# A fused attention, expert and dense kernel: the dense layer's token blocks change from six of 384 to 512, 256, 512, 512 and 512

## The chip, the cores and the metric

The kernel runs on one core of one Trainium2 chip. The metric is the device time of one execution in microseconds (us). Runs of the kernel before took 822.37 to 823.5 us, with a median of 822.54.

## What is computed

Four batches of eight heads go through windowed attention, the 2304 resulting tokens of 512 features through a layer of eight experts (each token to one), and every token through a dense layer with 2048 hidden features. Cut to what matters here, the last part is:

```python
def _moe2_ref(x, w_in, w_out):          # x: 2304 x 512
    h = x @ w_in                        # 512 x 2048
    beta = 1.0
    neg = h <= -beta
    pos = h >= beta
    g = np.where(pos, h, np.where(neg, 0.0, (h + beta) ** 2 / (4.0 * beta)))
    return (g @ w_out).astype(np.float32)   # 2048 x 512
```

w_in and w_out come as 64-bit floats; the kernel turns them into pairs of 32-bit values itself.

## The kernel before

There are three stages in one program. Attention and routing come first. Then the experts go one after another, largest first; expert e holds up to `CAPS[e]` tokens (384 down to 256), and its output, turned so that features lie on the partitions, is written to `ysT` in device memory, the tokens sorted by expert. The dense layer reads `ysT` in blocks of tokens. Last, rows are scattered to their places in the output by indirect DMA.

Every product is made of three matmuls: each operand is split into a high and a low part (`yh`/`yl`, `wc..h`/`wc..l`, `gh`/`gl`), and high by high, high by low and low by high are added up in PSUM.

**The dense layer before.** The 2304 tokens are six blocks of 384 (`HT`). The hidden features are 16 chunks of 128 (`ff`). A step of a block and a chunk has a first-layer part, `in_part` (L1532): 4 x 3 matmuls of 384 columns into a PSUM tile `ch` (L1539 to L1541), of which there are two, used in turn. Behind it stands the activation, as a chain over two engines: ScalarE makes `r` (L1545), VectorE squares it (L1547) and takes the maximum with `ch` (L1549), ScalarE rounds to `gh` (L1550), VectorE subtracts for `gl` (L1553). The chain's maximum is the last reader of `ch`. The second-layer part, `out_part` (L1576), has for each 128 tokens three matmuls of 512 columns that add to an output bank `o` (L1565 to L1567); there are six output banks. After chunk 15, `put` (L1578) copies a bank to SBUF, on ScalarE for even and on VectorE for odd tiles, and GpSimd issues the scatter (L1584).

The blocks go in four runs, the first two of two blocks each:

```python
    RUNS = (((0, 1), 0, 1), ((2, 3), 0, 1), ((4,), 0, 2), ((5,), TH, 2))
```

The last number of a run is its lag: the second-layer part of a chunk is issued so many chunks behind its first-layer part. The order on TensorE within a step of a pair is so: first-layer part of one block, of the other, then both second-layer parts of the chunk before. At the very start there is no chunk before, so four first-layer parts stand in a row.

A block is loaded by `load_y` (L1126, on the sync engine's DMA queue) and split into high and low parts by `split_y` (L1130, one ScalarE and one VectorE pass for each of four pieces).

**The conversion of the weights.** `conv64` (L1045) converts the 16 chunks of w_in and w_out. Half a chunk (w_in or w_out) costs VectorE four passes (L1059, L1061, L1064, L1052) and ScalarE two (`cvr`, L1043, and `wc..h`, L1067). It is a generator: what calls `next` on it sets where these passes stand in the queues. The first `NEARLY` = 5 chunks are converted during the expert stage, by `side_work` (L1393), two or three pieces for each hidden chunk of an expert. The others are advanced by `more` (L1527), five pieces in each `in_part` from the third on, so that one chunk is converted in each step of the first pair. The raw weights wait in two buffers; the load for two halves ahead is issued behind a half's second pass.

`py` is the pool of three buffers in which the experts' turned inputs (`new_xT`) and the dense blocks take turns.

Of the kernel before, what the change touches and what calls it, by code (L numbers as in the profile page):

```python
# [9 lines left out]
F32 = mybir.dt.float32  # L10
F32R = mybir.dt.float32r
BF16 = mybir.dt.bfloat16
I32 = mybir.dt.int32
# [7 lines left out]
P = 128  # L21
B, H, S, D = 4, 8, 576, 64
N = B * S
DM = H * D
E = 8
F = 1024
FF = 2048
# [3 lines left out]
CAP = 384  # L31
CAPS = (384, 376, 344, 314, 296, 286, 274, 256)
L2, L3 = 2, 4
NRAW, NW, LEAD = 6, 7, 5
NEARLY = 5
BIAS = {"V": 1.2}
# [11 lines left out]
CT = CAP // P  # L48
GT, HT = 768, 384
QF = S - S % P  # L50
# [6 lines left out]
def f(ap):  # L57
    return ap.bitcast(F32)
# [3 lines left out]
def fused_kernel(ctx, tc, qk, vT, v, emb, tau, w1, w2, win64, wout64, out):  # L62
    nc = tc.nc
# [957 lines left out]
    pcv = pool(ctx, "pcv", 1)  # L1021
    py = pool(ctx, "py", 3)
    wch = {}
# [97 lines left out]

    yt = {}

    def load_y(i):
        yl = py.tile([P, 4, CAP], F32R, tag="xl", name="yl")
        yh = py.tile([P, 4, CAP], F32R, tag="xh", name="yh")  # L1126
        nc.sync.dma_start(f(yl), ysT[:, i * HT:(i + 1) * HT].rearrange("(c p) s -> p c s", p=P))
        yt[i] = (yh, yl)
# [8 lines left out]
    with ExitStack() as bb:  # L1137
        pw = pool(bb, "pw", NW)
        px = pool(bb, "px", 2)
# [141 lines left out]
        def new_xT():  # L1281
            xh = py.tile([P, 4, CAP], F32R, tag="xh", name="xh")
            xl = py.tile([P, 4, CAP], F32R, tag="xl", name="xl")
            return xh, xl
# [229 lines left out]
    pg = pool(ctx, "pg", 3)  # L1514
    po = pool(ctx, "po", 2)
    ps_h = pool(ctx, "ps_ch", 2, space=PSUM)
# [4 lines left out]
    cv = conv64(range(NEARLY, FF // P), pcl)  # L1521
    TH = HT // P

    RUNS = (((0, 1), 0, 1), ((2, 3), 0, 1), ((4,), 0, 2), ((5,), TH, 2))
    outs, parts = {}, [0]

# [5 lines left out]
    def in_part(hf, ff):  # L1532
        parts[0] += 1
        w1h, w1l = wch[ff][:2]
        yh, yl = yt[hf]
        hp = ps_h.tile([P, HT], F32, tag="ch", name="ch")
        for c in range(4):
            o = slice(c * P, (c + 1) * P)
            nc.tensor.matmul(hp, w1h[:, o], yh[:, c], start=(c == 0), stop=False)  # L1539
            nc.tensor.matmul(hp, w1h[:, o], yl[:, c], start=False, stop=False)  # L1540
            nc.tensor.matmul(hp, w1l[:, o], yh[:, c], start=False, stop=(c == 3))  # L1541
        r = pg.tile([P, HT], F32, tag="r", name="r", bufs=2)
        a = pg.tile([P, HT], F32R, tag="gh", name="gh", bufs=4)
        b = pg.tile([P, HT], F32R, tag="gl", name="gl", bufs=4)
        nc.scalar.activation(r, hp, AF.Relu, bias=halfc, scale=0.5)  # L1545
        more()
        nc.vector.scalar_tensor_tensor(r, r, 1.0, r, op0=ALU.min, op1=ALU.mult)  # L1547
        more()
        nc.vector.tensor_tensor(r, hp, r, op=ALU.max)  # L1549
        nc.scalar.activation(a, r, AF.Copy)  # L1550
        more()
        more()
        nc.vector.tensor_tensor(b, r, f(a), op=ALU.subtract)  # L1553
        more()
        return a, b

    def out_tile(run, ff, gs, i, t):
        halves, b0, _ = run
        _, _, w2h, w2l = wch[ff]
        hf = halves[i]  # L1560
        gh, gl = gs[i]
        if ff == 0:
            outs[hf, t] = ps_o.tile([P, DM], F32, tag=f"o{b0 + i * TH + t}", name=f"o{b0 + i * TH + t}")
        o, out_ = slice(t * P, (t + 1) * P), outs[hf, t]
        nc.tensor.matmul(out_, gh[:, o], w2h, start=(ff == 0), stop=False)  # L1565
        nc.tensor.matmul(out_, gl[:, o], w2h, start=False, stop=False)  # L1566
        nc.tensor.matmul(out_, gh[:, o], w2l, start=False, stop=(ff == FF // P - 1))  # L1567
        if ff == FF // P - 1:
            put(hf, t)

    def out_part(run, ff, gs):
        for i in range(len(gs)):
            for t in range(TH):
                out_tile(run, ff, gs, i, t)

    def put(hf, t):  # L1576
        ot = po.tile([P, DM], F32, tag="ot", name="ot", bufs=3)
        if t % 2 == 0:  # L1578
            nc.scalar.activation(ot, outs.pop((hf, t)), AF.Copy)  # L1579
        else:  # L1580
            nc.vector.tensor_copy(ot, outs.pop((hf, t)))
        k = hf * TH + t
        nc.gpsimd.memset(gap, 0.0)  # L1583
# [6 lines left out]
    for run in RUNS:  # L1590
        halves, _, lag = run
        ahead = [h for h in (halves[0] + 2, halves[0] + 3) if len(halves) == 2 and h < N // HT]
        if ahead:
            load_y(ahead[0])
            coming = split_y(ahead[0])
        for ff in range(FF // P):
            gs = []
            for hf in halves:
                gs.append(in_part(hf, ff))
                if ahead and ff == FF // P - 1 and hf == halves[0]:  # L1600
                    del yt[hf]
                    load_y(ahead[1])
            todo.append((run, ff, gs))
            while len(todo) > lag:
                out_part(*todo.pop(0))
            if ff in (11, 12, 13, 14):
                next(coming, None)
        if ahead:
            for _ in split_y(ahead[1]):
                pass  # L1610

    for n, t in ((0, 0), (1, 0), (0, 1), (1, 1), (0, 2), (1, 2)):
        out_tile(*todo[n], 0, t)

# [44 lines left out]
```

## Time and profile before

| what | before |
|---|---|
| median of three runs | 822.54 us |
| profiled execution, its own time | 822.19 us |
| its span, first to last instruction | 820.5 us |
| TensorE busy, of the span | 806.9 us, 98% |
| weight loads busy | 749.8 us, 91% |
| VectorE busy | 516.9 us, 63% |
| ScalarE busy | 421.5 us, 51% |
| GpSimd busy | 137.7 us, 17% |
| mean granted clock of TensorE | 0.999 |

A busy time is the time in which at least one instruction of an engine ran. Matmuls overlap, and their ends are modelled, so a TensorE that is busy all the time can still lose time between the starts of its matmuls: starts are what to read. The names PE, DVE, ACT and POOL in the rows are TensorE, VectorE, ScalarE and GpSimd.

### The profile page before, as it was taken

The page shows a single profiled execution, that of the slowest core. Times are in us where ns is not written, and L with a number is a line of the kernel's source. Part 1 is how long each engine was busy: PE and PEld are TensorE (multiplying, and loading weights), DVE is VectorE, ACT ScalarE, POOL GpSimd, SP SyncE. Part 2 cuts the span into 40 slices and gives each one's busy share as a digit, 9 for nine tenths or more (in the row PEclk, how much of TensorE's full clock was granted, in tenths as well). Part 3 has the DMA queues.
Part 4 walks back from the last instruction along what each step waited for, and adds up shares of the span by engine and source line. Part 5 has one row for each costly group of instructions (what it writes and reads, how often), then busy time and mean ns, then how long its engine had stood idle before and what let it go on. Part 6 is the DMA issues. An engine that isn't in the chain of part 4 may idle for free.

```text
span 820.5 us, 14256 instructions
## 1 busy us (share of the span) xinstructions
PE 806.9 (98%) x5242; PEld 749.8 (91%) x5242; DVE 516.9 (63%) x1390; ACT 421.5 (51%) x881; POOL 137.7 (17%) x205
## 2 busy tenths in 40 slices
PE   9999999999999999999999999999999999999996
PEld 7999999869999999999998989999999999999995
DVE  7777767897667687777469898544343454344332
ACT  7879899856435466566345555333222333223221
POOL 5975664031110110100000000011000003001001
PEclk9999999999999999999999999999999999999999
DMA  9846942648645668776134332021000012001001
GB/s 335 308 158 237 330 160 71 227 160 277 202 159 166 216 216 276 241 235 198 62 116 128 129 122 84 1 100 55 0 1 1 1 40 77 1 1 40 1 0 39
DMA packets 59180, 106.03 MB, mean 129 GB/s; under 512 B 3942, under 2 KB 35686, under 8 KB 59104
## 3 DMA queue, kind: packets, MB, share of 16 engines
q1 hardware_dynamic: 55776, 95.15, 34.7%
q0 software_dynamic: 3328, 9.90, 3.5%
q8 instruction: 43, 0.70, 0.3%
q14 instruction: 33, 0.27, 0.1%
HBM read 90.42 MB, written 14.62 MB: 128 GB/s over the span
## 4 chain that ended last, share of the span: by engine, by line
issue 56%; PE 12%; POOL 2%; ACT 0%; DVE 0%; POOLq 0%; ACTq 0%
PE bh L1458 2%; POOL out L1584 2%; PE bh L1460 2%; PE bh L1459 2%; PE by L1447 2%; PE by L1449 2%; PE by L1448 2%; PE bx L1295 1%; ACT whi L555 0%; DVE wlo L560 0%; POOL gap L1583 0%; PE permp L1385 0%; POOLq L1655 0%; POOL xg L1166 0%; ACT yo L1497 0%
## 5 line engine op out<-in xcount | busy, mean ns | idle before, releaser
L1547 DVE SCALAR_TENSOR_TENSOR r<-r 128x384 f32<-128x384 f32 x96 | 53.4, 556 | 120.6 <-ACT r L1545 117.1
L1539 PE MATMUL ch<-yh,wc_0h 128*128 128x384 f32 x384 | 129.2, 336 | 0.0
L1541 PE MATMUL ch<-yh,wc_0l 128*128 128x384 f32 x384 | 129.1, 336 | 0.0
L1540 PE MATMUL ch<-yl,wc_0h 128*128 128x384 f32 x384 | 128.7, 335 | 0.0
L1545 ACT ACTIVATE r<-ch,halfc 128x384 f32<-128x384 f32 x96 | 55.2, 575 | 117.4 <-PE ch L1541 117.1
L1550 ACT ACTIVATE gh<-r 128x384 fp32r<-128x384 f32 x96 | 50.5, 526 | 123.4 <-DVE r L1549 123.4
L1566 PE MATMUL o<-wc_1h,gl 128*128 128x512 f32 x288 | 113.3, 393 | 0.1
L1567 PE MATMUL o<-wc_1l,gh 128*128 128x512 f32 x288 | 113.3, 393 | 0.0
L1565 PE MATMUL o<-wc_1h,gh 128*128 128x512 f32 x288 | 112.0, 389 | 0.0
L1584 POOL DMA_INDIRECT out<-ot,permu x18 | 17.5, 973 | 462.2 <-ACT ot L1579 458.9
L560 DVE TENSOR_TENSOR wlo<-wraw,whi 128x1024 fp32r<-128x1024 f32 x64 | 78.0, 1222 | 20.1 <-ACT whi L555 19.6
L1553 DVE TENSOR_TENSOR gl<-r,gh 128x384 fp32r<-128x384 f32 x96 | 53.4, 557 | 43.7 <-ACT gh L1550 42.6
L1458 PE MATMUL bh<-xh,whi 128*128 128x256 f32 (+6 forms) x256 | 80.2, 313 | 0.0
L1448 PE MATMUL by<-hl,whi 128*128 128x256 f32 (+6 forms) x256 | 77.5, 303 | 1.8 <-DVE hl L1464 1.8
L1447 PE MATMUL by<-hh,whi 128*128 128x256 f32 (+6 forms) x256 | 77.3, 302 | 0.0
L1449 PE MATMUL by<-hh,wlo 128*128 128x256 f32 (+6 forms) x256 | 77.3, 302 | 0.0
L1460 PE MATMUL bh<-xh,wlo 128*128 128x256 f32 (+6 forms) x256 | 77.1, 301 | 0.0
L1459 PE MATMUL bh<-xl,whi 128*128 128x256 f32 (+6 forms) x256 | 76.9, 301 | 0.0
L1539 PEld LDWEIGHTS ch<-yh,wc_0h 128*128 128x128 f32 x384 | 72.1, 188 | 2.9 <-DVE r L1549 0.3
L1540 PEld LDWEIGHTS ch<-yl,wc_0h 128*128 128x128 f32 x384 | 72.1, 188 | 2.5
L1541 PEld LDWEIGHTS ch<-yh,wc_0l 128*128 128x128 f32 x384 | 72.0, 188 | 0.0
L555 ACT ACTIVATE whi<-wraw 128x1024 fp32r<-128x1024 f32 x64 | 67.3, 1055 | 0.7 <-ACTq L1476 0.7
(270 smaller groups left out, 1718.9 us busy)
## 6 DMA issues: line engine op xcount, KB each, us to landing
wraw<-in_w SPq DMA_DIRECT2D x64, 512.0 KB, 4.6
rqk<-in_qk SPq DMA_DIRECT2D x30, 576.0 KB, 5.1
raw<-in_w_in SPq DMA_DIRECT2D x16, 512.0 KB
raw<-in_w_out SPq DMA_DIRECT2D x16, 512.0 KB, 4.7
vT<-in_vT SPq DMA_DIRECT2D x16, 288.0 KB, 2.8
yl<-ysT SPq DMA_DIRECT2D x6, 768.0 KB, 6.0
x_dram<-xt SPq DMA_DIRECT2D x8, 512.0 KB, 6.6
vt<-in_v SPq DMA_DIRECT2D x8, 438.0 KB, 6.8
```

Of the source, the lines that this page charges most:

```text
L1447: nc.tensor.matmul(y, w2h[:, o], hh[:, :cap], start=(ff == 0), stop=False)
L1448: nc.tensor.matmul(y, w2h[:, o], hl[:, :cap], start=False, stop=False)
L1449: nc.tensor.matmul(y, w2l[:, o], hh[:, :cap], start=False, stop=(ff == 7))
L1458: nc.tensor.matmul(hp, w1h[:, o], xh[:, c, :cap], start=(c == 0), stop=False)
L1459: nc.tensor.matmul(hp, w1h[:, o], xl[:, c, :cap], start=False, stop=False)
L1460: nc.tensor.matmul(hp, w1l[:, o], xh[:, c, :cap], start=False, stop=(c == 3))
L1539: nc.tensor.matmul(hp, w1h[:, o], yh[:, c], start=(c == 0), stop=False)
L1540: nc.tensor.matmul(hp, w1h[:, o], yl[:, c], start=False, stop=False)
L1541: nc.tensor.matmul(hp, w1l[:, o], yh[:, c], start=False, stop=(c == 3))
L1565: nc.tensor.matmul(out_, gh[:, o], w2h, start=(ff == 0), stop=False)
L1566: nc.tensor.matmul(out_, gl[:, o], w2h, start=False, stop=False)
L1567: nc.tensor.matmul(out_, gh[:, o], w2l, start=False, stop=(ff == FF // P - 1))
```

## The change

The dense layer gets five blocks of 512, 256, 512, 512 and 512 tokens. The first run has the blocks 0 and 1, the other runs one block each, with lag 1, the last with lag 2. Only 3 chunks of weights are converted in the expert stage. The experts' turned inputs move from `py` to the pool `px`; blocks get places of their own, the blocks 0 and 3 one, 1 one, 2 and 4 one in a pool `pz` that takes space the expert stage has left. The activations get two buffers for each block width, and in the last run four slots in the place of the blocks 0 and 3. The output copies use the conversion's `cvr` and `cva` buffers, two each, instead of three of their own. The six output banks are used in a circle over all 18 tiles of tokens.

```diff
-NEARLY = 5
+NEARLY = 3
...
-GT, HT = 768, 384
+SIZES = (512, 256, 512, 512, 512)
+GT = max(SIZES)
...
-    py = pool(ctx, "py", 3)
+    py = pool(ctx, "py", 1)
...
     def load_y(i):
-        yl = py.tile([P, 4, CAP], F32R, tag="xl", name="yl")
-        yh = py.tile([P, 4, CAP], F32R, tag="xh", name="yh")
-        nc.sync.dma_start(f(yl), ysT[:, i * HT:(i + 1) * HT].rearrange("(c p) s -> p c s", p=P))
+        t0, n = sum(SIZES[:i]), SIZES[i]
+        place, tag = ((py, 0), (py, 1), (late[0], 2), (py, 0), (late[0], 2))[i]
+        yl = place.tile([P, 4, n], F32R, tag=f"yl{tag}", name="yl")
+        yh = place.tile([P, 4, n], F32R, tag=f"yh{tag}", name="yh")
+        nc.sync.dma_start(f(yl), ysT[:, t0:t0 + n].rearrange("(c p) s -> p c s", p=P))
...
         def new_xT():
-            xh = py.tile([P, 4, CAP], F32R, tag="xh", name="xh")
-            xl = py.tile([P, 4, CAP], F32R, tag="xl", name="xl")
+            xh = px.tile([P, 4, CAP], F32R, tag="xh", name="xh")
+            xl = px.tile([P, 4, CAP], F32R, tag="xl", name="xl")
...
-    po = pool(ctx, "po", 2)
+    late[0] = pool(ctx, "pz", 1)
...
-    RUNS = (((0, 1), 0, 1), ((2, 3), 0, 1), ((4,), 0, 2), ((5,), TH, 2))
+    RUNS = ((0, 1), (2,), (3,), (4,))
+    first_tile = [sum(SIZES[:i]) // P for i in range(len(SIZES))]
...
-        hp = ps_h.tile([P, HT], F32, tag="ch", name="ch")
+        n = SIZES[hf]
+        hp = ps_h.tile([P, GT], F32, tag="ch", name="ch")[:, :n]
...
-        r = pg.tile([P, HT], F32, tag="r", name="r", bufs=2)
-        a = pg.tile([P, HT], F32R, tag="gh", name="gh", bufs=4)
-        b = pg.tile([P, HT], F32R, tag="gl", name="gl", bufs=4)
+        r = pg.tile([P, GT], F32, tag="r", name="r", bufs=2)[:, :n]
+        if hf == len(SIZES) - 1:
+            if ff == 0:
+                wide.extend(py.tile([P, 4, GT], F32R, tag=f"{t}0", name=f"{t}w") for t in ("yh", "yl"))
+            a, b = (w[:, ff % 4] for w in wide)
+        else:
+            a = pg.tile([P, n], F32R, tag=f"gh{n}", name="gh", bufs=2)
+            b = pg.tile([P, n], F32R, tag=f"gl{n}", name="gl", bufs=2)
...
         if ff == 0:
-            outs[hf, t] = ps_o.tile([P, DM], F32, tag=f"o{b0 + i * TH + t}", name=f"o{b0 + i * TH + t}")
+            bank = (first_tile[hf] + t) % 6
+            outs[hf, t] = ps_o.tile([P, DM], F32, tag=f"o{bank}", name=f"o{bank}")
...
     def put(hf, t):
-        ot = po.tile([P, DM], F32, tag="ot", name="ot", bufs=3)
+        ot = f(pcv.tile([P, 512], I32, tag=("cvr", "cva")[t % 2], name="ot", bufs=2))
...
     for run in RUNS:
-        halves, _, lag = run
-        ahead = [h for h in (halves[0] + 2, halves[0] + 3) if len(halves) == 2 and h < N // HT]
-        if ahead:
-            load_y(ahead[0])
-            coming = split_y(ahead[0])
+        halves, lag = run, 2 if run == RUNS[-1] else 1
+        if halves[-1] + 1 < len(SIZES):
+            load_y(halves[-1] + 1)
+            coming = split_y(halves[-1] + 1)
...
-    for n, t in ((0, 0), (1, 0), (0, 1), (1, 1), (0, 2), (1, 2)):
-        out_tile(*todo[n], 0, t)
+    for t in range(SIZES[-1] // P):
+        for step in todo:
+            out_tile(*step, 0, t)
```

The lines of after.py's functions stand some 2 to 13 lower than before's: the three first-layer lines L1539 to L1541 are L1545 to L1547 there. On TensorE, at the start of the dense layer, this is where the second first-layer part ends and the third begins, before (`ch_...` is the PSUM tile, `wc0_0h` the high part of w_in's chunk 0):

```order
L1539 MATMUL ch_7882<-yh_7548,wc0_0h_6156 128x384
L1540 MATMUL ch_7882<-yl_7547,wc0_0h_6156 128x384
L1541 MATMUL ch_7882<-yh_7548,wc0_0l_6157 128x384
L1539 MATMUL ch_7903<-yh_7214,wc1_0h_6391 128x384
L1540 MATMUL ch_7903<-yl_7213,wc1_0h_6391 128x384
L1541 MATMUL ch_7903<-yh_7214,wc1_0l_6392 128x384
```

And now:

```order
L1545 MATMUL ch_7834<-yh_7500,wc0_0h_6156 128x256
L1546 MATMUL ch_7834<-yl_7499,wc0_0h_6156 128x256
L1547 MATMUL ch_7834<-yh_7500,wc0_0l_6157 128x256
L1545 MATMUL ch_7855<-yh_7174,wc1_0h_6391 128x512
L1546 MATMUL ch_7855<-yl_7173,wc1_0h_6391 128x512
L1547 MATMUL ch_7855<-yh_7174,wc1_0l_6392 128x512
```

The second part is 256 columns wide and the third 512, where all were 384; the third part writes the `ch` buffer that the first part used.

On VectorE, late in expert 5, before (`hl` belongs to the experts' hidden layer, `wlo` to the conversion of expert weights, `cva` and `wc4_0l` to the dense layer's chunk 4):

```order
L1064 ISA cva_7105<-cva_7105,cvr_7049 128x1024
L1464 SCALAR_TENSOR_TENSOR hl_7169<-bh_7155,hh_7168 128x286
L560 TENSOR_TENSOR wlo_7185<-wraw_6914,whi_7184 128x1024
L1052 TENSOR_TENSOR wc4_0l_7104<-cva_7105,wc4_0h_7103 128x512
L1059 TENSOR_SCALAR cva_7193<-raw64_7005 128x512
L1464 SCALAR_TENSOR_TENSOR hl_7230<-bh_7216,hh_7229 128x274
L1499 COPY yo_7233<-by1_6828 128x286
L1499 COPY yo_7233<-by3_6830 128x286
L560 TENSOR_TENSOR wlo_7249<-wraw_6953,whi_7248 128x1024
L1061 SCALAR_TENSOR_TENSOR cva_7193<-raw64_7005,cva_7193 128x512
```

And now, from the same `hl` pass on:

```order
L1469 SCALAR_TENSOR_TENSOR hl_7134<-bh_7120,hh_7133 128x286
L562 TENSOR_TENSOR wlo_7150<-wraw_6907,whi_7149 128x1024
L1469 SCALAR_TENSOR_TENSOR hl_7190<-bh_7176,hh_7189 128x274
L1504 COPY yo_7193<-by1_6828 128x286
L1504 COPY yo_7193<-by3_6830 128x286
L562 TENSOR_TENSOR wlo_7209<-wraw_6942,whi_7208 128x1024
```

The passes L1064, L1052, L1059 and L1061 of the dense layer's chunk 4 are gone from here; those of chunk 3 ahead of them are gone likewise.

On VectorE in the first run, before, half a step with the conversion of half a chunk in it:

```order
L1547 SCALAR_TENSOR_TENSOR r_8038<-r_8038 128x384
L1059 TENSOR_SCALAR cva_8046<-raw64_7961 128x512
L1549 TENSOR_TENSOR r_8038<-ch_8025,r_8038 128x384
L1061 SCALAR_TENSOR_TENSOR cva_8046<-raw64_7961,cva_8046 128x512
L1064 ISA cva_8046<-cva_8046,cvr_8022 128x1024
L1553 TENSOR_TENSOR gl_8040<-r_8038,gh_8039 128x384
L1052 TENSOR_TENSOR wc6_1l_8045<-cva_8046,wc6_1h_8044 128x512
```

And now, a half step on block 0 (one on block 1 is the same with 256 columns in the passes on `r` and `gl`):

```order
L1559 SCALAR_TENSOR_TENSOR r_8041<-r_8041 128x512
L1061 TENSOR_SCALAR cva_8049<-raw64_7970 128x512
L1561 TENSOR_TENSOR r_8041<-ch_8028,r_8041 128x512
L1063 SCALAR_TENSOR_TENSOR cva_8049<-raw64_7970,cva_8049 128x512
L1066 ISA cva_8049<-cva_8049,cvr_8007 128x1024
L1565 TENSOR_TENSOR gl_8043<-r_8041,gh_8042 128x512
L1054 TENSOR_TENSOR wc5_0l_8048<-cva_8049,wc5_0h_8047 128x512
```

The passes stand in the same order, on 512 and 256 columns by turns. In a given step the conversion works on a chunk two lower than before.

## Rows read from the trace of the kernel before

**Rows 1.** First run, 20 us: busy PE, PEld, DVE, ACT, POOL; clock, DMA share, GB/s.

```profile
440.00:460.00 20.00, 20.00 (x101) 17.95 (x100) 18.23 (x35) 10.60 (x20) 0.00 (x0) 1.00 0.41 132
```

**Rows 2.** Page, groups by line: form, count, busy us, mean ns, idle us before.

```profile
L1539 PE MATMUL ch<-yh,wc_0h 128*128 128x384 f32 x384 | 129.2, 336 | 0.0
...
L1545 ACT ACTIVATE r<-ch,halfc 128x384 f32<-128x384 f32 x96 | 55.2, 575 | 117.4 <-PE ch L1541 117.1
...
L1565 PE MATMUL o<-wc_1h,gh 128*128 128x512 f32 x288 | 112.0, 389 | 0.0
```

**Rows 3.** Timeline of TensorE, pair step and single step: start us, length us, instruction.

```profile
501.26 0.33 PE L1539 MATMUL ch<-yh,wc_0h 128*128 128x384 f32 x1
...
505.45 0.39 PE L1565 MATMUL o<-wc_1h,gh 128*128 128x512 f32 x1
...
509.57 0.33 PE L1539 MATMUL ch<-yh,wc_0h 128*128 128x384 f32 x1
...
797.05 0.33 PE L1539 MATMUL ch<-yh,wc_0h 128*128 128x384 f32 x1
...
799.16 0.39 PE L1565 MATMUL o<-wc_1h,gh 128*128 128x512 f32 x1
...
801.24 0.33 PE L1539 MATMUL ch<-yh,wc_0h 128*128 128x384 f32 x1
```

**Rows 4.** The same view in the last expert.

```profile
404.82 0.28 PE L1458 MATMUL bh<-xh,whi 128*128 128x256 f32 x1
...
413.70 0.28 PE L1449 MATMUL by<-hh,wlo 128*128 128x256 f32 x1
```

**Rows 5.** Timeline, start of the dense layer, TensorE and VectorE.

```profile
413.82 0.34 PE L1539 MATMUL ch<-yh,wc_0h 128*128 128x384 f32 x1
...
417.37 0.56 DVE L1549 TENSOR_TENSOR r<-ch,r 128x384 f32<-128x384 f32 x1
...
417.98 0.44 PE L1539 MATMUL ch<-yh,wc_0h 128*128 128x384 f32 x1
418.26 0.34 PE L1540 MATMUL ch<-yl,wc_0h 128*128 128x384 f32 x1
```

**Rows 6.** Timeline, experts 5 and 6, TensorE and ScalarE, with idle time before in brackets.

```profile
342.76 0.29 PE L1447 MATMUL by<-hh,whi 128*128 128x286 f32 x1
343.10 0.40 PE L1448 MATMUL by<-hl,whi 128*128 128x286 f32 x1
...
344.81 0.63 ACT L1067 ACTIVATE wc_0h<-cva 128x512 fp32r<-128x512 f32 x1 [2.65 <-DVE cva L1064]
...
348.56 0.23 PE L1295 MATMUL bx<-ident,xg 18*128 18x18 f32 x1 [0.27 <-ACT xg L1344]
...
370.90 0.29 PE L1447 MATMUL by<-hh,whi 128*128 128x274 f32 x1
371.42 0.39 PE L1448 MATMUL by<-hl,whi 128*128 128x274 f32 x1 [0.22 <-DVE hl L1464]
```

**Rows 7.** Timeline of VectorE, half a step of the first run.

```profile
421.20 0.55 DVE L1547 SCALAR_TENSOR_TENSOR r<-r 128x384 f32<-128x384 f32 x1
...
423.19 0.69 DVE L1064 CUSTOM_DVE_ANT_0 cva<-cva,cvr 128x1024 uint16<-128x1024 uint16 x1
...
424.58 0.69 DVE L1052 TENSOR_TENSOR wc_0l<-cva,wc_0h 128x512 fp32r<-128x512 f32 x1 [0.23 <-ACT wc_0h L1067]
425.19 0.55 DVE L1547 SCALAR_TENSOR_TENSOR r<-r 128x384 f32<-128x384 f32 x1
```

**Rows 8.** Waits of ScalarE, first run: us in all, times, longest.

```profile
ACT cvr L1043 <- DMA raw<-in_w_in: 0.9, 2, 0.6
```

**Rows 9.** Timeline, output copies at a switch of runs and at the end.

```profile
553.34 0.60 ACT L1579 ACTIVATE ot<-o 128x512 f32<-128x512 f32 x1 [2.67 <-DMA out<-ot,permu]
...
811.53 0.60 ACT L1579 ACTIVATE ot<-o 128x512 f32<-128x512 f32 x1 [1.42 <-PE o L1567]
...
812.90 0.69 DVE L1581 COPY ot<-o 128x512 f32<-128x512 f32 x1 [2.20 <-PE o L1567]
```

More of the change, by code (lines that the diff above doesn't have):

```diff
@@ L1120, in overflow @@
                 nc.vector.tensor_scalar(rel_, rel_, -float(P), None, op0=ALU.add)
-    yt = {}
+    yt, late = {}, [None]
     def load_y(i):
-        yl = py.tile([P, 4, CAP], F32R, tag="xl", name="yl")
-        yh = py.tile([P, 4, CAP], F32R, tag="xh", name="yh")
-        nc.sync.dma_start(f(yl), ysT[:, i * HT:(i + 1) * HT].rearrange("(c p) s -> p c s", p=P))
+        t0, n = sum(SIZES[:i]), SIZES[i]
[3 more added lines that the diff above has]
+        nc.sync.dma_start(f(yl), ysT[:, t0:t0 + n].rearrange("(c p) s -> p c s", p=P))
         yt[i] = (yh, yl)
@@ L1521, in fused_kernel @@
     cv = conv64(range(NEARLY, FF // P), pcl)
-    TH = HT // P
-    RUNS = (((0, 1), 0, 1), ((2, 3), 0, 1), ((4,), 0, 2), ((5,), TH, 2))
-    outs, parts = {}, [0]
+    RUNS = ((0, 1), (2,), (3,), (4,))
+    first_tile = [sum(SIZES[:i]) // P for i in range(len(SIZES))]
+    outs, parts, wide = {}, [0], []
     def more():
@@ L1557, in out_tile @@
     def out_tile(run, ff, gs, i, t):
-        halves, b0, _ = run
+        halves = run
         _, _, w2h, w2l = wch[ff]
@@ L1572, in out_part @@
         for i in range(len(gs)):
-            for t in range(TH):
+            for t in range(SIZES[run[i]] // P):
                 out_tile(run, ff, gs, i, t)
     def put(hf, t):
-        ot = po.tile([P, DM], F32, tag="ot", name="ot", bufs=3)
+        ot = f(pcv.tile([P, 512], I32, tag=("cvr", "cva")[t % 2], name="ot", bufs=2))
         if t % 2 == 0:
@@ L1581, in put @@
             nc.vector.tensor_copy(ot, outs.pop((hf, t)))
-        k = hf * TH + t
+        k = first_tile[hf] + t
         nc.gpsimd.memset(gap, 0.0)
@@ L1599, in fused_kernel @@
                 gs.append(in_part(hf, ff))
-                if ahead and ff == FF // P - 1 and hf == halves[0]:
-                    del yt[hf]
-                    load_y(ahead[1])
             todo.append((run, ff, gs))
@@ L1607, in fused_kernel @@
                 next(coming, None)
-        if ahead:
-            for _ in split_y(ahead[1]):
-                pass
-    for n, t in ((0, 0), (1, 0), (0, 1), (1, 1), (0, 2), (1, 2)):
-        out_tile(*todo[n], 0, t)
+    for t in range(SIZES[-1] // P):
+        for step in todo:
+            out_tile(*step, 0, t)
 _OUTS = [((2304, 512), "float32")]
```

## The prediction

> **What bounds the kernel now.** I read the stretches by engine first. While the dense layer's first two blocks run, TensorE is busy for all 20 us of 440 to 460 at a granted clock of 1.00, which is the 2.4 GHz level, VectorE for 18.23 us and ScalarE for 10.60 us [rows 1]. So TensorE bounds it, with VectorE close behind. The groups by line say the same: 3 x 384 first-layer matmuls (`ch`) and 3 x 288 second-layer ones (`o`), with almost no idle time before them [rows 2]. The mean of 336 ns there is no cost: matmuls overlap, so a matmul costs the distance from its start to the next start. The next view gives those distances.
>
> In TensorE's timeline a pair step goes from 501.26 to 505.45 (24 matmuls of 384 columns, 4.19 us) and on to 509.57 (18 of 512 columns, 4.12 us); a single-block step has 12 in 2.11 us (797.05 to 799.16) and 9 in 2.08 us (to 801.24) [rows 3]. The differences cancel what belongs to the switch between parts: (4.19 - 2.11)/12 = 0.1733 us for 384 columns, (4.12 - 2.08)/9 = 0.2267 us for 512, and 0.03 + 0.04 = 0.07 us per step is left for its two switches. Expert matmuls of 256 columns start 74 times between 404.82 and 413.70, every 0.120 us [rows 4]. At 2.4 GHz the columns alone take 0.1067, 0.1600 and 0.2133 us. All three widths thus lie on one line: the columns, and about 13.4 ns per matmul whatever its width.
>
> **The change, part by part.**
>
> *Fewer, wider first-layer matmuls.* Six blocks of 384 need 6 x 16 x 12 = 1152; five blocks need 5 x 16 x 12 = 960. The columns are the same, and the 864 second-layer matmuls stay. Before: 32 pair steps of 24 x 0.1733 + 18 x 0.2267 + 0.07 = 8.31 us and 32 single steps of 4.19 us, 400.0 us. After: the first run (512 and 256 tokens) has 16 steps of 12 x 0.2267 + 12 x 0.120 + 18 x 0.2267 + 0.07 = 8.31 us, the same as before; three blocks of 512 have 48 steps of 24 x 0.2267 + 0.07 = 5.51 us; 397.5 us. **-2.5 us**, which is 192 x 13.4 ns. From below: if the line did not hold for `ch`, 0; I take it whole, since 512-column matmuls with the same kinds of operands are measured in the same steps. The Trainium skill, page "TensorE: Matmul & The Clock Gate", section "Wait — 56ns, not 53.3ns?", gives a warm matmul a fixed cost of about 2.5 ns beside its columns. By that page the term would be 192 x 2.5 ns = 0.5 us; the trace disagrees, with 13.4 ns.
>
> *A new wait at the start of the dense layer.* Two `ch` banks alternate, and in the first two steps no second-layer part stands between the first-layer parts. The third part, (block 0, chunk 1), starts when VectorE's maximum has read the first bank. Before, it was just in time: the first part begins at 413.82, its last matmul starts 11 x 0.1733 later, at 415.73, the maximum ends at 417.37 + 0.56 = 417.93, 2.20 us behind, and the part starts at 417.98, just when two parts of 2.08 us are over [rows 5]. Only the restart shows: 0.28 us to the next start, not 0.17 [rows 5]. Now the first part has 512 columns, but the one that should hide its chain has 256. The last matmul starts at 413.82 + 11 x 0.2267 = 416.31. The chain grows by two VectorE passes from about 0.55 to 0.69 us [rows 7, 9], by ScalarE's pass (0.575 us at 384 [rows 2], 0.60 for a 512-column copy [rows 9], at most a third more by columns: 0.02 to 0.19, I take 0.10) and by some 0.05 us of the matmul's own tail: 2.20 + 0.27 + 0.10 + 0.05 = 2.62. So the bank is free at 418.93 and TensorE goes on at 418.98, but would have been ready at 413.82 + 0.03 + 2.72 + 1.44 = 418.01. That is 0.97 us idle and 0.10 us restart, less some 0.2 us for the restarts that the old third and fourth part had: **+0.85 us**, between 0.5 and 1.6 (if the fourth part waits as well).
>
> *Two weight conversions leave the expert stage.* Chunks 3 and 4 were converted in experts 5 and 6 (counted from 0). There they held up TensorE: from the matmul at 342.76 it was 0.34 us to the next start, where 286 columns on the line above take 0.13; ScalarE had stood 2.65 us before `wc_0h` at 344.81, waiting for VectorE's `cva`, with the rest of its queue behind that, and the scaled rows `xg` then kept a transpose waiting 0.27 us at 348.56; at 370.90 it was 0.52 us, the matmul at 371.42 waiting for an `hl` that stood behind the `cva` passes [rows 6]. Against 0.13 us these are 0.21 + about 0.4 (the transpose and what it delays) + 0.39, and 0.1 for each of three restarts: 1.3 us. I take **-1.1 us**; bounds 0 (the waits fall on other work, such as the wider split of block 0 in expert 6, four VectorE passes of 0.69 in place of 0.55 us) and -1.3.
>
> *Two more conversions in the first run.* They go to VectorE, behind and between the passes on `ch`, in 13 steps instead of 11. Half a step on VectorE took 425.19 - 421.20 = 3.99 us, of which 1.39 us, from the last `cva` pass (423.19) to `wc_0l` (424.58), is the way through ScalarE, and hides the `gl` pass between [rows 7]. A 512 half grows by two passes of 0.135 us, a 256 half shrinks by as much: 4.26 + 3.72 = 7.98 us against TensorE's 8.31. So VectorE keeps up, and I cost it at nothing. In the three steps in which the last conversions meet the split of the next block, VectorE has one pass more, some 0.7 us, so it falls behind by 0.4 us a step, 1.1 us in all; a bank is needed again 8.31 - 2.75 - 2.6 = 3.0 us after its pass could be done. Converting chunk k two steps before its use, not four, leaves more than a step of 8.31 us.
>
> *Blocks in turn, and their buffers.* A block's output copies now use four buffers shared with the conversions instead of three of their own. At the first switch of runs ScalarE already waited 2.67 us for a scatter [rows 9], with no idle time before `o` matmuls [rows 2]; now the fifth and sixth copy wait instead of the fourth to sixth. Nothing. Blocks 2 to 4 rotate through the six output banks; each bank asked for was copied out at least a whole part (2.7 us) before. The loads of blocks 2, 3 and 4 each have a run's length. Nothing. In a single-block step the chain of `gl` (2.62 us as above, and a ScalarE and a VectorE pass of some 0.65 each, 3.9 us) has the next step's 5.5 us. Only at the very end is the last copy VectorE's 0.69 us, where it was ScalarE's 0.60 [rows 9]: **+0.1 us**.
>
> Sum: -2.5 + 0.85 - 1.1 + 0.1 = -2.65 us. The profiled execution took 822.19 us (its span, 820.5, and 1.7 around it), so 819.5; the median of the runs is 0.35 us above it, so I forecast **819.9 us**.
>
> **The rivals.** A measurement of this kernel can tell about 0.2%, 1.6 us, from no change.
> - *The gain stays under that.* The expert stage gives nothing back and the start costs its upper bound: -2.5 + 1.6 + 0.1 = -0.8, 821.7 us. For it: the first switch from expert to dense work is untried in this shape. Against: the stalls at 342.76 and 370.90 stand right behind the removed passes [rows 6].
> - *The per-matmul cost is not saved in `ch`*: its 13.4 ns would belong to what the first layer reads or writes and grow with its columns, so that fewer matmuls save nothing. Then the sum is 0.85 - 1.1 + 0.1 = -0.15 us, 822.4 us. The Trainium skill's page named above stands near this, with 0.5 us saved and 821.9 us. Against: three widths on one line [rows 3, 4].
> - *Slower: VectorE becomes the bound of the first run.* Place: the wait of ScalarE's `cvr` pass for the weight load, which came up twice, 0.6 us at the longest [rows 8]. The load is issued behind one half's `cva` pass and used in the next half; for the w_in loads that next half is now the short one, 0.27 us shorter. Up to 0.27 + 0.6 = 0.87 us a step makes VectorE's step 8.85 us; over 13 steps it falls 7.0 us behind, of which 3.0 are free: 4.0 us of stall, -2.65 + 4.0 = +1.35, 823.9 us. It decides from 0.33 + 3.0/13 = 0.56 us per step. Against: 0.9 us was the sum of all such waits in 21 passes [rows 8].
> - That the change is not what it says can be left out: TensorE's order, shown with the change, has the new shapes.
>
> **How the numbers follow.** My forecast 0.72; the small gain 0.14; the per-matmul cost not saved 0.06; slower 0.08. The forecast's own spread is the start (0.5 to 1.6) and the expert stage (0 to -1.3): 819.3 to 821.3, of which a small part, 0.04, is above 820.9. Faster than 0.2%: 0.68 and 0.03 of the small-gain case, 0.71. Same: 0.04, 0.11 and 0.06, and 0.01 from a mild form of the VectorE case, 0.22. Slower 0.07. The range takes the forecast down to 818.8, for stalls that I did not list, and reaches up to 822.4, over the two small-gain cases; left out are the VectorE case and the ends.
>
> **What would show it.** Right: 960 `ch` matmuls; single-block steps of 5.51 us and the first run's at 8.31; one gap of about 1 us in TensorE about 5 us after the first `ch` matmul; no gap of 0.2 us or more around chunks 3 and 4's old places in experts 5 and 6; dense layer about 399 us from first to last matmul start (now 400.0). Wrong: `ch` matmuls of 512 columns more than 0.23 us apart; further waits of `ch` matmuls on VectorE's maximum in the first run, or `cvr` waiting for loads in most steps; or gaps in the expert stage as large as before.

## The result, and the profile after

The changed kernel takes **816.07 us** (median of 4 runs, 815.68 to 816.37), the kernel before, run beside it, 822.64 us (822.37 to 823.5): a ratio of 0.9915 (95% interval 0.9903 to 0.9928), or 6.6 us less. The forecast was 819.9 us, 2.7 us less, with a range down to 818.8. The direction is right, the size is not: 3.9 us of the gain were not foreseen.

The groups by line of the changed kernel's page, which answer to [rows 2] (form, count, busy us, mean ns, idle us before and what ended it):

```profile
L1545 PE MATMUL ch<-yh,wc_0h 128*128 128x512 f32 (+1 forms) x320 | 117.8, 368 | 0.9 <-DVE r L1561 0.9
...
L1557 ACT ACTIVATE r<-ch,halfc 128x512 f32<-128x512 f32 x80 | 51.2, 641 | 119.3 <-PE ch L1547 118.8
...
L1579 PE MATMUL o<-wc_1h,gl 128*128 128x512 f32 x224 | 87.4, 390 | 0.2 <-DVE gl L1565 0.2
```

3 x 320 first-layer matmuls (`ch`) stand where 3 x 384 stood. TensorE idles before two groups now: 0.9 us before `ch`, as forecast, and 0.2 us before `o`, which was costed at nothing. The stretch that answers to [rows 1] (busy PE, PEld, DVE, ACT, POOL; clock, DMA share, GB/s):

```profile
440.00:460.00 20.00, 20.00 (x101) 16.99 (x101) 18.43 (x36) 11.30 (x20) 0.00 (x0) 1.00 0.40 127
```

TensorE still bounds the first run, at the 2.4 GHz level, and VectorE is as close behind it as it was: 18.43 us of 20, where it was 18.23.

I split the two profiled executions at the same places of the program. They took 822.19 and 816.37 us, 5.8 us apart where the medians are 6.6 apart; executions of one kernel differ by up to 1.1 us here (822.37 to 823.5). The rows are the first matmuls of experts 5, 6 and 7 in TensorE's timeline (start us, length us, instruction), first of the kernel before, then of the changed one:

```profile
336.57 0.29 PE L1458 MATMUL bh<-xh,whi 128*128 128x286 f32 x1
...
364.69 0.29 PE L1458 MATMUL bh<-xh,whi 128*128 128x274 f32 x1
...
390.79 0.29 PE L1458 MATMUL bh<-xh,whi 128*128 128x256 f32 x1
```

```profile
337.25 0.29 PE L1463 MATMUL bh<-xh,whi 128*128 128x286 f32 x1
...
364.35 0.29 PE L1463 MATMUL bh<-xh,whi 128*128 128x274 f32 x1
...
389.80 0.28 PE L1463 MATMUL bh<-xh,whi 128*128 128x256 f32 x1
```

With the first `ch` matmul (413.82 before [rows 5], 412.84 after), the last matmul (813.84 and 807.95) and the span's end (820.5 and 814.7), this gives:

| stretch | before | after | difference | forecast |
|---|---|---|---|---|
| start to the first matmul of expert 5 | 336.57 | 337.25 | +0.68 | 0 |
| experts 5, 6 and 7 | 77.25 | 75.59 | -1.66 | -1.1 |
| dense layer, first to last matmul start | 400.02 | 395.11 | -4.91 | -1.65 |
| last matmul to the span's end | 6.66 | 6.75 | +0.09 | +0.1 |

So nearly all of what was missed lies in the dense layer. Its single-block steps, in TensorE's timeline of the changed kernel:

```profile
701.74 0.39 PE L1545 MATMUL ch<-yh,wc_0h 128*128 128x512 f32 x1
...
702.42 0.39 PE L1545 MATMUL ch<-yh,wc_0h 128*128 128x512 f32 x1
...
704.46 0.39 PE L1578 MATMUL o<-wc_1h,gh 128*128 128x512 f32 x1
...
707.18 0.39 PE L1545 MATMUL ch<-yh,wc_0h 128*128 128x512 f32 x1
```

The step takes 5.44 us (701.74 to 707.18), not the forecast 5.51: 24 x 0.2267 and nothing else. The two halves are 2.72 us each, and three matmuls are 0.68 us from the first on. The **0.07 us "for its two switches"**, which every step before paid and which the forecast carried over, is gone. In the first run, where 512 and 256 columns alternate, a step takes 8.26 us, not 8.31:

```profile
500.81 0.39 PE L1545 MATMUL ch<-yh,wc_0h 128*128 128x512 f32 x1
...
509.07 0.39 PE L1545 MATMUL ch<-yh,wc_0h 128*128 128x512 f32 x1
```

Where did a step of the kernel before spend that 0.07 us? Between the rows of its single-block step that [rows 3] show stand these:

```profile
797.57 0.35 PE L1539 MATMUL ch<-yh,wc_0h 128*128 128x384 f32 x1
...
798.12 0.33 PE L1539 MATMUL ch<-yh,wc_0h 128*128 128x384 f32 x1
...
798.64 0.33 PE L1539 MATMUL ch<-yh,wc_0h 128*128 128x384 f32 x1
...
799.86 0.39 PE L1565 MATMUL o<-wc_1h,gh 128*128 128x512 f32 x1
...
800.55 0.39 PE L1565 MATMUL o<-wc_1h,gh 128*128 128x512 f32 x1
```

Read by threes, from 797.05: 0.52, 0.55, 0.52 and 0.52 us at 384 columns, then 0.70, 0.69 and 0.69 at 512, where three take 0.52 and 0.68 in a long row. There is no wait: the surplus is spread in small parts over several matmuls of each width. That made two theories for the experiments. **W (width)**: it is paid when the column count changes. **S (switch)**: it is paid at the change from one layer's part to the other's, whatever the columns.

The two waits of the changed kernel. First the start of the dense layer, TensorE:

```profile
412.84 0.40 PE L1545 MATMUL ch<-yh,wc_0h 128*128 128x512 f32 x1
...
415.58 0.28 PE L1545 MATMUL ch<-yh,wc_0h 128*128 128x256 f32 x1
...
416.90 0.28 PE L1547 MATMUL ch<-yh,wc_0l 128*128 128x256 f32 x1
...
418.04 0.50 PE L1545 MATMUL ch<-yh,wc_0h 128*128 128x512 f32 x1 [0.86 <-DVE r L1561]
418.38 0.40 PE L1546 MATMUL ch<-yl,wc_0h 128*128 128x512 f32 x1
```

From 416.90 to 418.04 are 1.14 us where a start takes 0.12, and the restart to 418.38 is 0.11 over 0.23: 1.13 us (forecast 1.07). Then the change from the first run to the third block, TensorE:

```profile
557.09 0.40 PE L1578 MATMUL o<-wc_1h,gh 128*128 128x512 f32 x1
557.65 0.50 PE L1579 MATMUL o<-wc_1h,gl 128*128 128x512 f32 x1 [0.17 <-DVE gl L1565]
557.99 0.40 PE L1580 MATMUL o<-wc_1l,gh 128*128 128x512 f32 x1
```

0.33 and 0.11 us over the 0.23 of a start: 0.44 us, not forecast. Its cause is in the rows of GpSimd and ScalarE:

```profile
548.67 1.02 POOL L1598 DMA_INDIRECT out<-ot,permu  x1 [213.03 <-ACT ot L1593]
```

```profile
553.56 0.60 ACT L1593 ACTIVATE ot<-o 128x512 f32<-128x512 f32 x1 [4.69 <-DMA out<-ot,permu]
```

The second block's copies take the buffers that the first block's scatters still read. The first scatter starts at 548.67, and the copy that needs its buffer goes at 553.56, **4.89 us** later. Behind the copy, ScalarE's and VectorE's passes for the next chunk come late, and at 557 `gl` is missing. Taken together, the dense layer's -4.91 us is -2.57 (192 matmuls x 13.4 ns), +0.93 (start, less 0.2 for the old restarts), +0.44 (change of runs), and a rest of -3.71 us: the surplus in the steps. By steps it is 64 x 0.065 before and 16 x 0.02 after, 3.8 us. Added up over all starts of the layer, what stands above the bare matmuls and is no wait or restart is 4.17 us before and 0.42 us after, 3.75 us less. A last stop, near 810.3 before and 803.1 after, is the same in both (0.36 and 0.33 us).

### The profile page after: what moved, and what is told of

The parts are those of the page before. It is cut to its first block, busy times and chain, and to the rows that moved or that the text cites. A ratio compares the mean times of both kernels' runs of the same rounds, so it can differ in the third digit from the quotient of the medians.

```text
span 814.7 us, 13748 instructions
## 1 busy us (share of the span) xinstructions
PE 800.6 (98%) x5050; PEld 715.8 (88%) x5050; DVE 512.6 (63%) x1341; ACT 414.7 (51%) x842; POOL 138.0 (17%) x205
## 4 chain that ended last, share of the span: by engine, by line
PE 58%; issue 10%; DVE 2%; ACT 1%; POOL 1%; DMA 0%; POOLq 0%; DVEq 0%; ACTq 0%
PE ch L1545 6%; PE ch L1547 6%; PE ch L1546 6%; PE o L1579 6%; PE o L1580 6%; PE o L1578 6%; PE bh L1463 4%; PE bh L1465 3%; PE by L1452 3%; PE by L1454 3%; PE bh L1464 3%; PE by L1453 3%; PE bx L1300 1%; POOL out L1598 1%; DMA wraw<-in_w 0%
## 5 line engine op out<-in xcount | busy, mean ns | idle before, releaser
L1559 DVE SCALAR_TENSOR_TENSOR r<-r 128x512 f32<-128x512 f32 x80 | 51.0, 637 | 118.8 <-ACT r L1557 117.3
L1545 PE MATMUL ch<-yh,wc_0h 128*128 128x512 f32 (+1 forms) x320 | 117.8, 368 | 0.9 <-DVE r L1561 0.9
L1546 PE MATMUL ch<-yl,wc_0h 128*128 128x512 f32 (+1 forms) x320 | 117.7, 368 | 0.0
L1547 PE MATMUL ch<-yh,wc_0l 128*128 128x512 f32 (+1 forms) x320 | 117.7, 368 | 0.0
L1557 ACT ACTIVATE r<-ch,halfc 128x512 f32<-128x512 f32 x80 | 51.2, 641 | 119.3 <-PE ch L1547 118.8
L1579 PE MATMUL o<-wc_1h,gl 128*128 128x512 f32 x224 | 87.4, 390 | 0.2 <-DVE gl L1565 0.2
L1578 PE MATMUL o<-wc_1h,gh 128*128 128x512 f32 x224 | 87.4, 390 | 0.0
L1580 PE MATMUL o<-wc_1l,gh 128*128 128x512 f32 x224 | 87.1, 389 | 0.0
L1562 ACT ACTIVATE gh<-r 128x512 fp32r<-128x512 f32 x64 | 37.1, 579 | 97.7 <-DVE r L1561 96.3
L1545 PEld LDWEIGHTS ch<-yh,wc_0h 128*128 128x128 f32 x320 | 60.3, 188 | 11.6 <-DVE r L1561 1.1
L1468 ACT ACTIVATE hh<-bh 128x256 fp32r<-128x256 f32 (+6 forms) x64 | 26.9, 420 | 85.0 <-PE bh L1465 83.3
L1547 PEld LDWEIGHTS ch<-yh,wc_0l 128*128 128x128 f32 x320 | 60.3, 188 | 10.0
```

## The experiments

### One width throughout, in the kernel before; two widths, in the changed one

```diff
-        nc.tensor.matmul(out_, gh[:, o], w2h, start=(ff == 0), stop=False)
+        n = DM if ff in (0, FF // P - 1) else 384
+        nc.tensor.matmul(out_[:, :n], gh[:, o], w2h[:, :n], start=(ff == 0), stop=False)
...
```

The same cut in both kernels, for chunks 1 to 14; it leaves out what these chunks add to the last 128 output columns. In the kernel before it makes both layers 384 columns wide; in the changed one it puts 384 beside 512, where the single-block steps were all 512. The parts, the order and the waits of TensorE stay.

> The kernel before, with the second-layer matmuls of chunks 1 to 14 cut from 512 to 384 columns (the last 128 output columns miss those chunks). All matmuls of a step then have one width. Theory W: the 0.07 us per step that the prediction called the price of two switches of parts comes with a change of the column count from one matmul to the next. Then a single-block step takes (12 + 9) x 0.1733 = 3.64 us and a pair step after the first run 7.28 us, with no start-to-start distance above 0.176 us inside them. Rival S: it belongs to blocks of 384 and their buffers, or to the switch from first to second layer as such. Then 3.71 and 7.35 us, with the slow first matmuls of each part still there. The first run may be held by VectorE (7.98 us per step), so the whole time, some 787 us by W and 790 us by S, says less than the steps.

Measured: 785.24 us, in one run. A single-block step in TensorE's timeline:

```profile
741.62 0.34 PE L1566 MATMUL o<-wc_1h,gh 128*128 128x384 f32 x1
...
743.18 0.34 PE L1539 MATMUL ch<-yh,wc_0h 128*128 128x384 f32 x1
...
745.26 0.33 PE L1566 MATMUL o<-wc_1h,gh 128*128 128x384 f32 x1
```

9 matmuls in 1.56 us and 12 in 2.08: 3.64 us, 21 x 0.1733, with no surplus. The parts still alternate, so S falls.

> The changed kernel with the same cut (second-layer matmuls of chunks 1 to 14 on 384 columns, the last 128 output columns miss those chunks), so that its single-block steps change width twice, 512 to 384 and back, where they had one width. Theory W: a step takes 12 x 0.2267 + 12 x 0.1733 + about 0.065 = 4.87 us, and the first six to nine matmuls behind each switch stand further apart than the others. Rival S: 4.80 us and no such pattern. Whole time about 787 us by W, 785 us by S, with the first run held by VectorE in both.

Measured: 789.69 us, in one run. The step:

```profile
652.62 0.33 PE L1579 MATMUL o<-wc_1h,gh 128*128 128x384 f32 x1
...
654.73 0.39 PE L1545 MATMUL ch<-yh,wc_0h 128*128 128x512 f32 x1
...
657.49 0.33 PE L1579 MATMUL o<-wc_1h,gh 128*128 128x384 f32 x1
```

12 of 384 in 2.11 us (bare 2.08) and 12 of 512 in 2.76 (bare 2.72): the surplus of 0.07 us is back, in a kernel that had none. **W holds**, from both sides. The same execution has a control: where one block ends and the next begins, the second layer kept 512 columns, and there a step with 512 throughout takes 5.44 us again (625.00 to 630.44 in TensorE's timeline), while the steps around it take 4.87. The whole times missed the expectation (some 787 us for both by W). That of this kernel isn't only that of its steps: with shorter matmuls TensorE now waits for VectorE in the first run (6.6 us before `ch` between 430 and 540; 3.1 us in the kernel before with this cut).

### How the surplus goes with the widths

```diff
+        n = DM if ff in (0, FF // P - 1) else (DM, DM, 448, 256, 480)[hf]
```

> The changed kernel, with the second-layer matmuls of chunks 1 to 14 at 448 columns in the third block, 256 in the fourth and 480 in the fifth; it leaves out the contribution of those chunks to the last 64, 256 and 32 output columns there. First-layer matmuls stay at 512 columns, so a step is 12 matmuls of 512 and 12 of fewer. With 226.7 ns for 512 columns and 13.4 ns + n/2.4 for n, a step that pays nothing for its two changes of column count is 12 x (226.7 + 200.1) = 5.12 us at 448, 12 x (226.7 + 120.1) = 4.16 us at 256 and 12 x (226.7 + 213.4) = 5.28 us at 480. Theory 'by difference' (0.065 us a step at a difference of 128 columns, in proportion): 5.15, 4.29 and 5.30 us. Theory 'per change' (0.065 us a step whatever the difference): 5.19, 4.23 and 5.35 us. Theory 'the pair 512 and 256 is free' (the first run of the changed kernel alternates these two and its steps had only 0.02 us over the bare matmuls): 5.19, 4.16 to 4.18, and 5.35 us. All three: whole kernel about 816.1 - 14 x (0.32 + 1.28 + 0.16) = about 791.5, less or more by the excess, up to 2 us.

Measured: 793.74 us, in one run. A step beside 448, 256 and 480 columns, in this order (first `ch`, first `o`, next first `ch`):

```profile
565.43 0.39 PE L1545 MATMUL ch<-yh,wc_0h 128*128 128x512 f32 x1
...
568.16 0.36 PE L1579 MATMUL o<-wc_1h,gh 128*128 128x448 f32 x1
...
570.60 0.39 PE L1545 MATMUL ch<-yh,wc_0h 128*128 128x512 f32 x1
...
642.48 0.40 PE L1545 MATMUL ch<-yh,wc_0h 128*128 128x512 f32 x1
...
645.22 0.28 PE L1579 MATMUL o<-wc_1h,gh 128*128 128x256 f32 x1
...
646.66 0.40 PE L1545 MATMUL ch<-yh,wc_0h 128*128 128x512 f32 x1
...
726.40 0.39 PE L1545 MATMUL ch<-yh,wc_0h 128*128 128x512 f32 x1
...
729.12 0.38 PE L1579 MATMUL o<-wc_1h,yhw 128*128 128x480 f32 x1
...
731.73 0.39 PE L1545 MATMUL ch<-yh,wc_0h 128*128 128x512 f32 x1
```

5.17, 4.18 and 5.33 us, that is 0.05, 0.02 and 0.05 over the bare matmuls (the other steps with the same widths are within 0.02 us of these); with 384 it was 0.07. 'By difference' falls at 256 (4.29 expected), and so does 'per change' (4.23). The theory that the pair 512 and 256 is nearly free holds there; it came from the first run of the changed kernel and is now seen in another place. At 448 and 480 no theory met the number (5.19 and 5.35, or 5.15 and 5.30). The 512-column half is nearly bare there, 2.73 and 2.72 us; the surplus lies in the other half, 2.44 us where 12 matmuls at 13.4 ns and their columns are 2.40, and 2.61 where they are 2.56. Whether it is the change of width or these widths themselves that cost it, this run can't tell: "13.4 ns and the columns" is shown for rows of 256, 384 and 512 columns alone.

### The conversions out of experts 5 and 6

```diff
-NEARLY = 5
+NEARLY = 3
```

In the kernel before, alone: three chunks of the dense layer's weights are converted in the expert stage instead of five.

> The kernel before with only 3 chunks of weights converted in the expert stage, the one part of the change that touches experts 5 and 6. Theory: the stalls of TensorE in these experts come from the conversion of chunks 3 and 4; then expert 5 goes from 28.12 to about 27.1 us, expert 6 from 26.10 to about 25.5, and the whole to about 821.0 us. Rival: the stalls belong to the experts' own passes and the gain came from the new pools or from chance; then the experts keep their lengths and the whole stays at 822.6 us; if the two conversions more made VectorE hold up the first run, it would be above that.

Measured: 820.87 us, ratio 0.9975 (0.9966 to 0.9985). The first matmuls of experts 5 and 6, and of the dense layer:

```profile
337.10 0.29 PE L1458 MATMUL bh<-xh,whi 128*128 128x286 f32 x1
...
364.20 0.29 PE L1458 MATMUL bh<-xh,whi 128*128 128x274 f32 x1
...
412.68 0.34 PE L1539 MATMUL ch<-yh,wc_0h 128*128 128x384 f32 x1
```

Expert 5 takes 27.10 us, as in the changed kernel (337.25 to 364.35), and from its start to the dense layer there are 75.58 us (75.59 in the changed kernel, 77.25 before). The term is this edit's alone, and it is -1.7 us.

### The two waits, together and one by one

```diff
+        if parts[0] == 3:
+            hp = ps_o.tile([P, GT], F32, tag="o5", name="o5")[:, :n]
+        else:
             hp = ps_h.tile([P, GT], F32, tag="ch", name="ch")[:, :n]
...
+        if hf == 1:
+            ot = f(pcv.tile([P, 512, 2], I32, tag="raw64", name="ot", bufs=2).rearrange("p a o -> p (a o)")[:, :512])
+        else:
             ot = f(pcv.tile([P, 512], I32, tag=("cvr", "cva")[t % 2], name="ot", bufs=2))
```

The first edit lets the third first-layer part write an accumulator bank that the second layer does not use yet. The second gives the second block's copies other buffers.

> The changed kernel with its two waits taken away: the third first-layer part of the dense layer writes an output bank that is still free, instead of the first ch bank, and the copies of block 1 go to the raw weights' buffers instead of waiting for scatters of block 0. Theory: the gap of TensorE at 416.9 (about 1.0 us with its restart) is the wait for VectorE's maximum on the first ch bank, and the gap at 557 (about 0.45 us) comes from copies that wait for scatters and hold up the activation chain; both go, and the time falls by 1.4 us, to about 814.7 us. Rival: another wait stands right behind each (the chain of block 1, the gl of the first part); then less than half of it is seen, 815.4 us or more.

Measured: 814.86 us, ratio 0.9898 (0.9883 to 0.9913), as the theory had it. Neither wait is in its trace.

> The changed kernel, with only the third first-layer part writing a bank of the second layer's accumulators that is still free at that point (the wait at the start of the dense layer is taken out; the copies of the second block stay in the two shared buffers). Theory: the two waits are separate, so this gives back the first alone: 1.0 us idle and 0.1 us of restart, 816.07 - 1.1 = 815.0, and the wait at the change to the third block stays at about 0.5 us with its restart. Rival: the dense layer that starts a microsecond earlier meets the copies' scatters a microsecond more out of step, or VectorE's lag behind the first run carries the wait on: 815.5 to 816.

Measured: 813.95 us, ratio 0.9894 (0.9879 to 0.991): lower than either theory had it. In TensorE's timeline the third part follows at once, in the bank `o5`:

```profile
416.18 0.28 PE L1550 MATMUL ch<-yh,wc_0l 128*128 128x256 f32 x1
...
416.30 0.40 PE L1548 MATMUL o<-yh,wc_0h 128*128 128x512 f32 x1
```

But the wait at the change of runs is gone too, although its buffers are as they were. The same two rows of GpSimd and ScalarE:

```profile
546.78 1.02 POOL L1601 DMA_INDIRECT out<-ot,permu  x1 [211.86 <-ACT ot L1596]
```

```profile
551.14 0.60 ACT L1596 ACTIVATE ot<-o 128x512 f32<-128x512 f32 x1 [4.15 <-DMA out<-ot,permu]
```

From scatter to copy it is 4.36 us here, 0.53 less than in the changed kernel, and TensorE's wait and restart there were 0.44. The copies still wait (4.15 us); they are only no longer late enough. So this wait stands on the edge, and how long the first scatter holds its buffer decides it. In the kernel before, the copy that waits for it (553.34 [rows 9]) goes only 2.87 us behind it:

```profile
550.47 1.02 POOL L1584 DMA_INDIRECT out<-ot,permu  x1 [215.50 <-ACT ot L1579]
```

The DMA view shows what differs. The queue that it calls "instruction" moves one packet of 0.02 MB near there. In the kernel before it starts at 549.10 and takes 0.94 us, and is over before the scatter starts. In the changed kernel it starts at 550.25, in the middle of the scatter, and takes 1.76 us; here at 548.37 and 1.25 us. In both the copy goes 1.5 to 1.6 us behind the packet's end (552.01 to 553.56, 549.62 to 551.14), and so it does in the two versions of the changed kernel above that have narrower second-layer matmuls (548.54 to 550.10 and 552.22 to 553.77). By this reading the packet accounts for the 0.53 us. It rests on these profiles; no run moved the packet, and why its length differs stays open.

The dense layer takes 393.45 us from first to last matmul start, 1.66 less than in the changed kernel; the version with both edits takes 393.46. The other 0.71 us by which this profile is shorter lie ahead of expert 5, where the edit changes nothing, so a part of the low time is not shown to be the edit's.

> The changed kernel, with only the copies of the second block going to two further buffers, so that they need not wait for the first block's scatters (the wait at the start of the dense layer stays). Theory: 816.07 - 0.45 = 815.6, with no idle TensorE at the change from the first two blocks to the third, and the start wait as it was (0.9 us for the chain's record). Rival: the banks that the third block takes are waited for because of the copies' engines, not their buffers, and the wait stays: 816.1.

Measured: 815.3 us, ratio 0.9912 (0.9898 to 0.9925). By the ratio it can't be told from the changed kernel (0.9915), but its trace is as the theory had it: `o` matmuls stand 0.23 us apart at the change of runs, and the start wait remains. The versions with the first edit, with and without the second, can't be told apart by their ratios (0.9894 and 0.9898) nor by their dense layers, so **the first edit alone is enough** here. Its four runs (813.75 to 814.12 us) all lie below those of the changed kernel (815.68 to 816.37), taken at another time; the intervals of the two ratios still touch (up to 0.991, from 0.9903).

### Fewer changes of width in the expert stage

If a change of width costs time, the experts pay it as well: four times an expert TensorE leaves its matmuls for transposes of 128 columns.

```diff
-            for c in range(4):
-                xp = ps_x.tile([P, CAP], F32, tag="xp", name="bx")
+            for c0 in (0, 2):
+                xps = []
+                for c in (c0, c0 + 1):
...
+                yield
                 yield
```

> The version with both waits taken out, and in the expert stage the transposes of the next expert's tokens are issued for two 128-wide slices of the model dimension at once instead of one, so TensorE goes from the experts' matmuls to 128-column transposes and back 2 times an expert instead of 4 (7 experts, 14 fewer excursions). Theory: each excursion costs about 0.2 us beyond its transposes, of which the change of column count is at least half; 14 x 0.1 to 0.2 = 1.4 to 2.8 us less than the version with both waits taken out (814.9), so 812.1 to 813.5. Rival: the cost belongs to the wait for the tokens and to each transpose, or ScalarE's two copies one after the other hold back the activation that the next matmuls wait for: 814.9 or above.

> The version with both waits taken out, again, beside the one with paired transposes on the same chip: 814.9 (813.6 to 815.2), 0.9898 of the kernel before.

Measured: 817.22 us with paired transposes, 814.80 without (ratios 0.9925 and 0.9898). **The theory fell.** Experts 3 and 4 alone gained, 0.1 us each (30.04 and 28.38 us, where it was 30.16 and 28.47). Experts 1 and 2 lost 0.9 and 1.05 us (36.58 and 34.73, where it was 35.68 and 33.68). The group of TensorE's other user of the transposes' banks, experts 1 and 2, with pairs and without:

```profile
L1390 PE MATMUL permp<-poa,poc 128*128 128x18 bf16 x36 | 2.1, 171 | 1.9 <-DVE xl L1295 1.7
```

```profile
L1390 PE MATMUL permp<-poa,poc 128*128 128x18 bf16 x36 | 2.1, 172 | 0.1
```

With pairs both banks are taken at once, and the matmuls that sort the token numbers wait for VectorE's `xl` to free one: 1.8 of the 1.95 us. Experts 5 and 6 lost 0.5 and 0.4 us; where, I didn't follow. In the two experts that gained, an excursion saved gave 0.05 us, not 0.1 to 0.2. Whether the change of width has any part in what an excursion costs, these runs don't show.

## Why the prediction was wrong in size, point by point

- **The step that failed** is the sum of the steps after the change: "three blocks of 512 have 48 steps of 24 x 0.2267 + 0.07 = 5.51 us". The 0.07 us was read rightly off the steps before and given a name, "its two switches", that no row had shown. It belongs to the change between 384 and 512 columns. Steps of one width don't pay it (5.44 us), and 512 beside 256 pay 0.02 (8.26 us, forecast 8.31). 48 x 0.07 + 16 x 0.05 = 4.2 us were thereby carried over that were not there (3.8 with the unrounded 0.065 us a step). The starts by threes in the kernel before show that it is no wait at a switch; the forecast took only the two ends of each part. What in the chip makes the spacing wider stays open.
- **Fewer matmuls, -2.5 us**: right. 512-column `ch` matmuls start 0.2267 us apart (701.74 to 704.46 is 12 of them). The Trainium skill, page "TensorE: Matmul & The Clock Gate", section "Wait — 56ns, not 53.3ns?", gives a warm matmul its columns and about 2.5 ns, 215.7 ns at 512 columns. The trace disagrees here as well: 226.7 ns. That section has one fixed cost per matmul; the 0.02 to 0.07 us that a step with two widths pays stands beside it.
- **The start wait, +0.85 us**: right in mechanism, place and size (1.13 us in all, 0.93 net).
- **The conversions, -1.1 us**: right in mechanism, undersized: -1.66, beyond its bound of -1.3. The one-edit run puts all of it on `NEARLY`.
- **Two more conversions in the first run, 0**: right. But the rival's first sign came: ScalarE's `cvr` pass waited for the weight loads 4.3 us in all between 412 and 560, where it was 0.9 [rows 8]:

```profile
L1045 ACT ACTIVATE cvr<-raw 128x512 int32<-128x512 uint32 x25 | 16.7, 668 | 4.3 <-DMA raw<-in_w_in 4.3
```

  In 25 passes that is 0.17 us a pass, 0.34 a step; the rival needed 0.56 a step to decide. TensorE's steps stayed at 8.26 us.
- **Copies through shared buffers, "Nothing"**: wrong by 0.44 us. The forecast saw that ScalarE would wait for a scatter, but took over the wait of the kernel before (2.67 us), counted how many copies wait and not how far behind that puts the passes queued after them. The scatter held its buffer for 4.89 us instead of 2.87, and the wait was 4.69 us. No row of the kernel before showed that; with 0.53 us less, the term was nothing (the first edit alone).
- **The end, +0.1 us**: right (+0.09).
- **The first 337 us, 0**: +0.68 in the profiled execution: the first expert starts at 182.33, not 181.85, and expert 2 takes 33.68, not 33.48 us. The kernel before with 384 columns in both layers, whose edit touches the dense layer alone, starts expert 5 at 337.33, which is +0.76, so a difference of this size comes without the change. The changed kernel with the first edit alone is back at 181.82 and 33.48, with both edits at 182.48 and 33.68. What sets these values stays open.
- **The spread**: its named bounds (start 1.6, experts 0) add up to 821.7 us, not 821.3; the miss lies on the other side.

## What to carry to other kernels

When a fit leaves a remainder per step, find the rows that hold it before carrying it over: starts read three by three tell a wait (one long distance) from a slower stretch (many slightly long ones). In a loop whose matmuls alternate between widths, try one width for both, or 512 beside 256; 384 beside 512 cost 0.07 us a step here, 4.2 us in all. The change took back some 3.7 of them, half again as much as the fewer matmuls saved. And when blocks change size, look for the first parts, where nothing stands between two users of an alternating pair of banks: a bank that is idle at that point cost nothing and took away a wait of 1.1 us.

## What the hardware did that I had not expected

- After a change of column count, matmuls are spaced wider for a while without waiting for anything: 0.55 us for the second three of 384 columns instead of 0.52, 0.70 and 0.69 for threes of 512 instead of 0.68. It comes back in every step (4.18 to 4.19 us in all single-block steps read between 690 and 800), and it doesn't grow with the difference: 0.07 us a step for 384 beside 512, 0.02 for 256 beside 512. What in the chip does this, no run here shows.
- Beside 512, matmuls of 480 columns are spaced 217 ns apart ((731.73 - 729.12)/12) and those of 448 203 ns ((570.60 - 568.16)/12), 3 to 4 ns over the line through 256, 384 and 512.
- A scatter of 128 rows of 2 KB held its buffer for 2.87 us from its start on GpSimd in the kernel before, and for 4.36 to 4.89 us where a 0.02 MB packet of the instruction queue fell into it. GpSimd itself was busy 1.02 us of that.
